# A recurrent attention kernel: the softmax weights of the first two units transposed by VectorE, dense rows laid out as 128 half rows

## The chip, the cores and the metric

The kernel runs on one core of a Trainium2 chip. The metric is the device time of one execution in microseconds, the median of several runs. A profile of one execution goes with it: TensorE is PE (its weight loads PEld), VectorE DVE, ScalarE ACT, GpSimd POOL, and SyncE SP, which issues most DMAs.

## The reference

Two layers of memory-augmented attention and two dense layers alternate, each behind a layernorm and with a residual, over 2048 rows of 512 (bf16):

```python
def _A_ref(x, mem0, Wq, Wk, Wv, Wo, seg_len):     # 32 heads of 128, 8 memory rows, segments of 32
    for s in range(n_seg):                         # 64 segments, one after the other
        h = jnp.concatenate([mem, xs], axis=1)     # 8 memory rows and 32 rows of the segment
        q, k, v = (jnp.einsum('btd,dhe->bhte', h, W) for W in (Wq, Wk, Wv))
        scores = jnp.einsum('bhqe,bhke->bhqk', q, k) * scale
        scores = jnp.where(mask[None, None], scores, -1000000000.0)
        p = _softmax(scores, axis=-1)
        o = jnp.einsum('bhqk,bhke->bhqe', p, v)
        o = jnp.einsum('bhte,hed->btd', o, Wo)
        mem = o[:, :M, :]                          # the next segment's memory
        outs.append(o[:, M:, :])
...
x = x + _A_ref(_layernorm(x), ...)
x = x + _B_ref(_layernorm(x), B_w1, B_w2)          # relu(x @ w1) @ w2, 512 to 1376 to 512
x = x + _A_ref(_layernorm(x), ...)
x = x + _B_ref(_layernorm(x), B_w1, B_w2)
```

The weights are the same in both passes. The memory ties each segment to the one before it.

## The kernel before, in words

The kernel walks in 66 steps. Step k works on segment k of the first attention layer and segment k - 2 of the second one at once (`DELTA` is 2), so that the 40 rows (8 of memory, 32 of the segment) of both stand side by side as 80 columns in `HT`. Steps 0, 1, 64 and 65 hold one layer only; 62 steps hold both.

In a step the 32 heads are cut into five units (`UNITS`): units 0 to 2 take eight heads each, units 3 and 4 four each. `queries_keys` forms q and k of four heads in 16 matmuls of 80 columns into a PSUM bank, and an eviction by ScalarE or VectorE brings them to SBUF as bf16. `scores` makes the 40 x 40 scores (matmuls of 40 columns in half the array's width), and then a chain runs: VectorE adds the mask (`block`, which also brings the scores out of PSUM), takes the maximum (`top`), subtracts it (`sub`), ScalarE applies the exponential, VectorE sums (`total`) and inverts (`recip`), and VectorE or GpSimd multiplies into the bf16 tile `P` (`mul`). PE transposes P against the identity (`turn`), and two masked evictions (`keep`, one for each half of the partitions, with the other half set to zero through `half`) write `PT`. `attend` multiplies PT with the values: those of the first layer in `V0`, of the second in `vw`. `project` sums all heads into one bank (`st`), and its eviction gives the next step's memory columns in `HT` and the rows `OX`.

`finish` takes the rows on. A DMA transpose on SP's queue turns OX into `y`; VectorE adds it to the residual `x` (`xg`), 64 rows of 512: 32 of each layer. `dense_layer` normalises them, turns them on PE (`turned`, four matmuls of 64 columns), runs w1 with the relu and w2. The totals give `Z`; its first 32 rows are normalised and turned for the second layer's HT two steps later, and kept as its residual (`carry`); its last 32 rows are the output (`narrow`, `store`). Row loads (`load_group`), late values of later groups (`prepare_late`, `late_values`) and copies of values into V0 (`place_values`) fill in between.

The order of all engines' instructions is worked out beforehand by a planner. `plan.op` names the engines an operation may run on, a cost for each, and what it reads and writes. PE's order is a list sorted by the numbers in `PLACE` (its phases: the first steps, the middle, the last ones); other operations get a due time from what follows them, shifted by `AHEAD`; and `Plan.order` gives each to the engine and place where it can start first. `PAIRED` names matmul groups that may run as two half-width halves, which saves a change of array width when their neighbours are half-width ones. Each engine's queue then runs in that order, and a late operation holds up all that stand behind it on its engine. In the change `PLACE`, `AHEAD`, `PAIRED` and `LOOK` have new values throughout, so nearly every instruction may change its place.

Of the kernel before, what the change touches and what calls it, by code (L numbers as in the profile page):

```python
# [8 lines left out]
BF = mybir.dt.bfloat16  # L9
# [21 lines left out]
LOOK = 0.0763052  # L31
PERIOD = 26.155362
PLACE = {
# [185 lines left out]


def t_dve(n, rate=1):
    return 0.07 + 1.042e-3 * n / rate


PART, MASKED = {ACT: 0.13, DVE: 0.10}, {ACT: 0.11, DVE: 0.065}
XBAR = 0.5, 0.2, 2.6


def t_pool(n):
    return 0.06 + 2.2e-3 * n  # L230

# [1144 lines left out]
```

## Time and profile before

| | before |
|---|---|
| median of 3 runs | 1590.69 us (1588.59 to 1592.59) |
| the profiled execution | span 1588.6 us, which is the fastest of the three runs |
| PE busy | 1569.5 us, 99% of the span |
| weight loads busy | 1411.1 us, 89% |
| DVE / ACT / POOL busy | 68% / 73% / 20% |
| granted TensorE clock | 0.998 of full |

An engine's busy time is the union of its instructions' spans. In a list of groups each line reads: source line, engine, operation, output <- input, shapes, count | busy us, mean ns of one | idle time just before, and what ended it. A matmul's shape carries the part of the array that it uses: 128*128 is the whole, 128*64 half its columns. In a timeline the first two columns are the start and the length of a merged group. In a table of stretches each engine has its busy us and its number of instructions, then come the granted clock, the DMA share and GB/s.

### The profile page before, as it was taken

Reading aid. Unit: us, or ns where it says so; the run is one execution under the profiler, and the core shown is the slowest. Engines: PE = TensorE matmul, PEld = TensorE weight load, DVE = VectorE, ACT = ScalarE, POOL = GpSimd, SP = SyncE. Lnnn points to the kernel's source line nnn. Section 1 sums busy time; section 2 is a strip of 40 time slices with the busy share of each in tenths; the row PEclk is TensorE's granted clock in tenths of the full one; section 3 lists DMA queues with packets and bytes.
Section 4 is the critical chain, followed back from the end, with each engine's and each line's share of the span. In section 5 each row is a group of like instructions: output and inputs, shape, how many; then the busy total and the mean of one; then the engine's idle time right before and its main releaser. Section 6 shows DMA issues by size and latency. Waiting matters only on the chain.

```text
span 1588.6 us, 100346 instructions
## 1 busy us (share of the span) xinstructions
PE 1569.5 (99%) x45458; PEld 1411.1 (89%) x45458; DVE 1082.3 (68%) x2957; ACT 1165.2 (73%) x3073; POOL 314.3 (20%) x667
## 2 busy tenths in 40 slices
PE   8999999999999999999999999999999999999998
PEld 5689999999999989999989999999998998898887
DVE  4566766766776776686676677677667667667665
ACT  4667777777777777777777777777777777777774
POOL 5112112212112212121121221211211121112110
PEclk9999999999999999999999999999999999999999
DMA  9711111111111111111111111111111111111100
GB/s 371 243 44 30 26 33 32 29 35 37 25 39 31 35 29 33 29 32 40 26 36 27 35 26 42 37 26 38 25 35 28 33 33 29 33 25 22 28 21 9
DMA packets 76540, 70.89 MB, mean 45 GB/s; under 512 B 50920, under 2 KB 62416, under 8 KB 76112
## 3 DMA queue, kind: packets, MB, share of 16 engines
q1 hardware_dynamic: 70096, 44.14, 13.1%
q0 software_dynamic: 4992, 19.40, 3.4%
q8 instruction: 356, 5.83, 1.6%
q10 hardware_dynamic: 1024, 0.93, 0.2%
q14 instruction: 72, 0.59, 0.1%
HBM read 31.53 MB, written 9.96 MB: 26 GB/s over the span
## 4 chain that ended last, share of the span: by engine, by line
PE 97%; DMA 1%; DVE 1%; POOL 1%; ACT 0%; issue 0%; DVEq 0%; POOLq 0%
PE work L726 40%; PE st L726 19%; PE fill L1048 16%; PE fill L726 8%; PE fill L821 5%; PE work L1217 5%; PE work L1133 4%; DMA xg<-in_A_x_dram 0%; DMA y<-OX 0%; DMA w_sb<-in_B_w_dram 0%; ACT HT L982 0%; POOL Wo_sb L537 0%; PE fill L711 0%; DVE ln L749 0%; POOL ln L736 0%
## 5 line engine op out<-in xcount | busy, mean ns | idle before, releaser
L726 PE MATMUL work<-HT,Wq_sb 128*128 128x80 bf16 (+2 forms) x10400 | 361.8, 201 | 3.1 <-ACT HT L982 3.1
L726 PE MATMUL work<-HT,Wk_sb 128*128 128x80 bf16 (+2 forms) x10416 | 362.7, 201 | 0.8 <-ACT HT L982 0.8
L726 PEld LDWEIGHTS <-Wq_sb 128*128 128x128 bf16 (+1 forms) x10400 | 330.9, 104 | 20.8 <-issue 6.0
L726 PE MATMUL st<-OT,Wo_sb 128*128 128x80 bf16 (+1 forms) x8448 | 345.5, 201 | 0.0
L726 PEld LDWEIGHTS <-Wk_sb 128*128 128x128 bf16 (+1 forms) x10416 | 327.1, 104 | 17.3 <-issue 2.0
L726 PEld LDWEIGHTS <-Wo_sb 128*128 128x128 bf16 x8448 | 315.7, 100 | 13.0 <-issue 12.7
L1048 PE MATMUL fill<-Wv_sb,HT 128*64 128x512 bf16 x2112 | 273.6, 381 | 1.1 <-DVE HT L984 1.0
L982 ACT CAST kT<-work 128x320 bf16<-128x320 f32 (+1 forms) x523 | 218.3, 418 | 68.6 <-PE work L726 31.1
L982 ACT CAST qT<-work 128x320 bf16<-128x320 f32 (+1 forms) x516 | 215.7, 418 | 67.5 <-PE work L726 47.2
L1198 ACT ACTIVATE PT<-work,half 128x160 bf16<-128x160 f32 (+1 forms) x515 | 231.3, 463 | 20.1 <-PE work L726 12.7
L982 ACT CAST OT<-work 128x320 bf16<-128x320 f32 (+1 forms) x461 | 186.2, 420 | 50.7 <-PE work L1217 50.6
L982 ACT CAST vw<-fill 128x512 bf16<-128x512 f32 x229 | 134.1, 586 | 113.3 <-PE fill L1048 109.8
L1144 DVE TENSOR_TENSOR es<-work,maskb 128x320 f32<-128x320 f32 (+2 forms) x330 | 136.2, 413 | 99.7 <-PE work L1133 93.2
L924 DVE TENSOR_TENSOR xg<-xg,y 64x512 f32<-64x512 f32 x65 | 44.2, 680 | 227.2 <-DMA y<-OX 226.6
L731 POOL TENSOR_SCALAR ln<-ln 32x1 f32<-32x1 f32 (+2 forms) x159 | 46.6, 293 | 566.7 <-DVE ln L752 561.0
L1155 ACT ACTIVATE es<-es 128x320 f32<-128x320 f32 (+2 forms) x330 | 136.1, 413 | 24.4 <-DVE es L1151 16.2
L1048 PEld LDWEIGHTS <-HT 128*64 128x64 bf16 x2112 | 98.9, 110 | 57.0 <-DVE HT L984 1.2
L1151 DVE TENSOR_TENSOR es<-es,mx 128x320 f32<-128x320 f32 (+2 forms) x330 | 136.3, 413 | 4.9
L1148 DVE TENSOR_REDUCE mx<-es 128x8 f32<-128x320 f32 (+2 forms) x330 | 133.9, 406 | 5.4
L1158 DVE TENSOR_REDUCE sm<-es 128x8 f32<-128x320 f32 (+2 forms) x330 | 133.4, 404 | 5.1 <-ACT es L1155 2.2
L1175 DVE TENSOR_TENSOR P<-es,sm 128x320 bf16<-128x320 f32 (+1 forms) x269 | 126.9, 472 | 3.3
L1133 PEld LDWEIGHTS <-qT 128*40 128x40 bf16 x4096 | 93.3, 97 | 35.6 <-ACT qT L982 13.6
(96 smaller groups left out, 2164.8 us busy)
## 6 DMA issues: line engine op xcount, KB each, us to landing
V<-vw SPq DMA_DIRECT2D x248, 48.0 KB
V<-vh SPq DMA_DIRECT2D x120, 64.0 KB
Wq_sb<-in_A_Wq_dram POOLq DMA_DIRECT2D x2, 2048.0 KB, 23.2
Wk_sb<-in_A_Wk_dram POOLq DMA_DIRECT2D x2, 2048.0 KB, 28.6
Wo_sb<-in_A_Wo_dram POOLq DMA_DIRECT2D x2, 2048.0 KB, 39.4
vh<-vg SPq DMA_DIRECT2D x32, 128.0 KB
xb<-in_A_x_dram SPq DMA_DIRECT2D x16, 128.0 KB
Wv_sb<-in_A_Wv_dram POOLq DMA_DIRECT2D x1, 2048.0 KB, 13.2
```

The costliest lines, as they stand in the source:

```text
L726: nc.tensor.matmul(out_[u:v, :], lhsT=lhsT[:, u:v], rhs=rhs, start=start, stop=stop, tile_position=(0, u), **more)
L821: nc.tensor.matmul(yp[64 * u:64 * u + 64, 0:256], lhsT=hT[:, fc, :], rhs=w2_sb[:, fc, 256 * u:256 * u + 256], start=(fc == 0), stop=(fc == ...
L982: nc.scalar.copy(out=out_, in_=in_)
L1048: nc.tensor.matmul(vp[64 * b:64 * b + 64, :], lhsT=cols(c4), rhs=Wv_sb[:, c4, n * 512:(n + 1) * 512], start=(c4 == 0), stop=(c4 == NC4 - 1 ...
L1133: nc.tensor.matmul(v[64 * g2:64 * g2 + L, a, i, b, :], lhsT=qT[:, hi, a * L:(a + 1) * L], rhs=kT[:, hi, a * L:(a + 1) * L], start=True, st ...
L1144: nc.vector.tensor_tensor(out=flat(es[:, A]), in0=flat(sp[:, A]), op=ALU.add, in1=maskb[:, a_lo:a_hi, :].unsqueeze(2).to_broadcast([128, n ...
L1148: nc.vector.tensor_reduce(out=mx[:, As], in_=es3(), axis=AX.X, op=ALU.max)
L1151: nc.vector.tensor_tensor(out=es3(), in0=es3(), op=ALU.subtract, in1=mx[:, As].unsqueeze(2).to_broadcast([128, ns * na, L]))
L1155: nc.scalar.activation(out=es[:, A], in_=es[:, A], func=ACTF.Exp, scale=SCALE)
L1158: nc.vector.tensor_reduce(out=sm[:, As], in_=es3(), axis=AX.X, op=ALU.add)
L1175: (nc.gpsimd if eng == POOL else nc.vector).tensor_tensor(out=o, in0=flat(es[:, A]), op=ALU.mult, in1=sm[:, As].rearrange("p (a s) -> p a ...
L1198: nc.scalar.activation(out=o, in_=i, func=ACTF.Copy, scale=half[:, b:b + 1])
```

## The change

- Units 0 and 1 (`BLOCKED`) are no longer transposed by PE. Their scores are stored so that the two heads of a pair alternate element by element; two bf16 make one 32-bit word. VectorE's `transpose` then turns blocks of 32 x 32 words from P into the unit's `es` buffer, and narrow copies (`stay`: 64 partitions; `shift`: two copies of 32 partitions that change their quarter) by ScalarE or GpSimd put the pieces into PT, whose other half stays zero from the start. The mask add reads the scores of a pair alternately; `mul` is two instructions; `attend` reads PT with a step of two elements.
- Units 2 to 4 keep the old way, into tiles named `PM`.
- The residual rows, y, Z and the dense rows are 128 half rows of 256 columns where they were 64 (or 32) rows of 512. The layernorm exchanges the two halves' statistics by two small copies (`swap`); the turns are two matmuls each; the copies `widen` and `carry` become two each, the totals one, the store two DMAs; the DMA transpose of OX has half the size.
- The row load of a group waits until the turn of OX has been issued (`("out", ...)`).
- `y`, `ob` and `xe` now lie in the free halves of `xg`, `none` and `mb0` in P tiles; `es` has three buffers instead of two; the mask has one copy for each pair.
- Two of the planner's POOL costs, and its tables, have new values.

```diff
-LOOK = 0.0763052
+LOOK = 0.1074729
...
+BLOCKED = (0, 1)
...
+def t_moved(eng, n):
+    return 0.205 + 0.86e-3 * n if eng == ACT else 0.20 + 1.08e-3 * n
...
-    PL = 256 + LK[1]
-    Pt = [sb(f"P{p}", [128, 2 * PL]) for p in range(4)]
+    PL = [256 + (2 if p in BLOCKED else 1) * LK[1] for p in range(4)]
+    Pt = [sb(f"P{p}", [128, 2 * PL[p]]) for p in range(4)]
...
+    spare = [t[:, 256:512].bitcast(BF) for t in xg]
+    p_y, p_ob, p_xe = Pool([spare[0][:, 0:256]]), Pool([spare[0][:, 256:512]]), Pool([spare[1]], True)
...
-    p_es = ring("es", 2, [128, 8 * L], F32)
-    p_PT = ring("PT", 3, [128, 2, 4, 2, L])
+    p_es = ring("es", 3, [128, 8 * L], F32)
+    p_PT, p_PM = ring("PT", len(BLOCKED), [128, 4, 2, 128]), ring("PM", 2, [128, 2, 4, 2, L])
...
-            plan.op(POOL, 0.80, power, r=["half"], w=[ln])
+            plan.op(POOL, 0.95, power, r=["half"], w=[ln])
...
+    def layernorm_halves(x, keys, quick=False):
+        ln, xn = p_ln.buf(), p_xr.buf()
+        R = slice(0, 128)
+        def stats():
+            nc.vector.bn_stats(out=ln[:, 0:6], in_=x[:, :])
+        def swap(eng):
+            for u in range(2):
+                copy_on(eng, ln[64 * u:64 * u + 64, 8:14], ln[64 - 64 * u:128 - 64 * u, 0:6])
+        def aggr():
+            nc.vector.bn_aggr(out=ln[:, 6:8], in_=ln[:, :].rearrange("p (s f) -> p s f", s=2)[:, :, 0:6])
+        def norm():
+            nc.vector.tensor_scalar(out=xn[:, 0:256], in0=x[:, :], scalar1=ln[:, 6:7], scalar2=ln[:, 7:8],
+                                    op0=ALU.subtract, op1=ALU.mult)
+        plan.op(DVE, t_dve(256), stats, r=keys, w=[ln])
+        plan.op((ACT, DVE), (0.2, 0.2), swap, w=[ln])
+        plan.op(DVE, 0.11, aggr, w=[ln])
+        rstd(ln, R, quick)
+        plan.op(DVE, 0.26, norm, r=[ln, *keys], w=[xn])
+        return xn
...
+    def turned(xn, n, columns, copies, blocks=NC4):
...
+            for c4 in range(blocks):
+                across(cols, tp[:, c4 * wide:(c4 + 1) * wide], xn[:, c4 * 128:(c4 + 1) * 128], columns)
...
-        xnT, xn = p_xm.buf(), layernorm(x, keys, slice(0, n), last)
-        turned(xn, n, ident[:, 0:n], [(NC4 * n, lambda: xnT[:, :, :], same, [], [xnT])])
+        xnT, xn = p_xm.buf(), layernorm_halves(x, keys, last)
+        turned(xn, n, ident[:, :], [(NC4 * n, lambda: xnT[:, :, :], same, [], [xnT])], 2)
...
-        plan.op(SP, 0.78, load, r=[("taken", 4 * g - 4)], w=[xb], lag=2.45)
+        plan.op(SP, 0.78, load, r=[("taken", 4 * g - 4), ("out", 4 * g - 4)], w=[xb], lag=2.45)
...
-            plan.op(SP, XBAR[0] + XBAR[1] * NC4, turn, r=["ox"], w=[y], lag=XBAR[2])
-        plan.op(DVE, t_dve(512), add, r=[y], w=keys)
+            plan.op(SP, XBAR[0] + XBAR[1] * 2, turn, r=["ox"], w=[y, ("out", k), *([("xv", 1), ("xv", 3)] if k == 0 else [])],
+                    lag=XBAR[2])
+        plan.op(DVE, t_dve(256), add, r=[y], w=keys)
...
+    def moved(eng, out_, in_):
+        if eng == ACT:
+            nc.scalar.copy(out=out_, in_=in_)
+        else:
+            nc.gpsimd.tensor_copy(out=out_, in_=in_)
 
...
-                            nc.tensor.matmul(v[64 * g2:64 * g2 + L, a, i, b, :], lhsT=qT[:, hi, a * L:(a + 1) * L],
+                for i in range(nx):
+                    for s in range(2):
+                        for t in range(2):
+                            g, b = (s, t) if blocked else (t, s)
+                            (qT, kT), hi = (qk[b], 2 * i + g) if nx == 2 else (qk[0], 2 * b + g)
+                            nc.tensor.matmul(v[64 * t:64 * t + L, a, i, s, :], lhsT=qT[:, hi, a * L:(a + 1) * L],
...
         def block():
-            nc.vector.tensor_tensor(out=flat(es[:, A]), in0=flat(sp[:, A]), op=ALU.add,
-                                    in1=maskb[:, a_lo:a_hi, :].unsqueeze(2).to_broadcast([128, na, ns, L]))
+            if blocked:
+                nc.vector.tensor_tensor(out=es[:, A].rearrange("p (j k s) -> p j k s", k=L, s=2), op=ALU.add,
+                                        in0=sp[:, A].rearrange("p (j s k) -> p j k s", k=L, s=2),
+                                        in1=maskb[:, mine, :].unsqueeze(3).to_broadcast([128, nj, L, 2]))
+            else:
+                o, i = (t[:, A].rearrange("p (j s k) -> p j s k", s=2, k=L) for t in (es, sp))
+                nc.vector.tensor_tensor(out=o, in0=i, op=ALU.add,
+                                        in1=maskb[:, mine, :].unsqueeze(2).to_broadcast([128, nj, 2, L]))
 
...
+        pieces = [(a, a + 1) for a in range(a_lo, a_hi)] if nx == 2 else [(a_lo, a_hi)]
+        def mul():
+            for a0, a1 in pieces:
+                o = P[:, :].rearrange("p (a c) -> p a c", a=2)[:, a0:a1, 128 * xs[0]:128 * (xs[-1] + 1)]
+                o = (o[:, 0, :] if nx == 2 else o).rearrange("p x (k g) -> p x k g" if nx == 1 else "p (x k g) -> p x k g", k=64, g=2)
+                j = slice((a0 - a_lo) * nx, (a1 - a_lo) * nx)
+                nc.vector.tensor_tensor(out=o[:, :, 0:L, :], in0=e_spread()[:, j, :, :], op=ALU.mult,
+                                        in1=by_head(sm)[:, j, :].unsqueeze(2).to_broadcast([128, nx * (a1 - a0), L, 2]))
+        plan.op(DVE, len(pieces) * (0.04 + t_dve(n / len(pieces))), mul, r=[es, sm], w=where)
         PT = p_PT.buf()
-        plan.op(PE, nx * na * 0.0358, turn, r=[*[("P", p, b, x) for b in range(2) for x in xs], "ident"], w=[tp, PT],
-                tile=EITHER, count=nx * na)
+        def turn():
+            nc.vector.transpose(out=es[:, 0:64 * nj].rearrange("p (j k) -> p j k", k=64),
+                                in_=P[:, 0:512].bitcast(F32).rearrange("p (j k) -> p j k", k=64)[:, mine, :])
+        def turned_pairs():
+            return es[:, 0:64 * nj].rearrange("p (j k) -> p j k", k=64), PT[:, 0:nj, :, :].bitcast(F32)
+        plan.op(DVE, 0.09 + 1.06e-3 * 64 * nj, turn, r=[*where, "PT0"], w=[es, PT])
         for b in range(2):
...
+            def stay(eng, b=b):
+                i, o = turned_pairs()
+                R = slice(64 * b, 64 * b + 64)
+                moved(eng, o[R, :, b, 0:L], i[R, :, 0:L])
+            def shift(eng, b=b):
+                i, o = turned_pairs()
+                for c, w in ((0, L - 32), (1, 32)):
+                    R, T = slice(64 * b + 32 * c, 64 * b + 32 * c + 32), slice(64 * b + 32 - 32 * c, 64 * b + 64 - 32 * c)
+                    moved(eng, o[R, :, b, 32 - 32 * c:32 - 32 * c + w], i[T, :, 32 * c:32 * c + w])
+            plan.op((ACT, POOL), (t_moved(ACT, L * nj), t_moved(POOL, L * nj) + 0.07), stay, r=[es, PT], w=[(PT, b)])
+            plan.op((ACT, POOL), tuple(t_moved(e, (L - 32) * nj) + t_moved(e, 32 * nj) for e in (ACT, POOL)), shift,
+                    r=[es, PT], w=[(PT, b)])
...
+        def spread(a, i, g):
+            if p in BLOCKED:
+                return PT[:, (a - a_lo) * nx + i, :, :].rearrange("p b (q g) -> p b q g", g=2)[:, :, 0:L, g]
+            return PT[:, a, 2 * i + g, :, :]
 
...
-                                             rhs=PT[:, a, 2 * i + h2, :, :], start=True, stop=True, tile_position=(0, u))
+                                             rhs=spread(a, i, h2), start=True, stop=True, tile_position=(0, u))
```

More of the change, by code (lines that the diff above doesn't have):

```diff
@@ L692, in prepare, with zero_last @@
         plan.op(DVE, 0.12, keep, r=[tp], w=["mem0T"])
+        def zero_last():
+            nc.vector.memset(Pt[2][:], 0.0)
+        plan.op(DVE, 0.30, zero_last, w=[mb0, *[("P", 2, b, x) for b in range(2) for x in range(2)]])
         plan.op(DVE, 0.12, place, r=["mem0T"], w=[("HTm", 0)])
@@ L902, in finish @@
         last = k == nsteps - 1
[L903 removed]
+        x, keys = x_of[k % 2], [("x", k % 2, a) for a in range(2)]
         if 0 in act:
@@ L937, in total @@
         def total(to):
-            for u in range(2):
-                cs = slice(256 * u, 256 * u + 256)
-                nc.vector.tensor_tensor(out=to[RB, cs], in0=x[RB, cs], in1=yp[64 * u:64 * u + 64, 0:256], op=ALU.add)
+            nc.vector.tensor_tensor(out=to[:, :], in0=x[:, :], in1=yp[:, 0:256], op=ALU.add)
         def total_x():
@@ L1193, in scores @@
-        for b in range(2):
-            def keep(eng, b=b):
-                o = PT[:, a_lo:a_hi, 0:2 * nx, b, :]
-                i = tp[:, A].rearrange("p (a g q) -> p a g q", g=2 * nx, q=L)
-                if eng == ACT:
-                    nc.scalar.activation(out=o, in_=i, func=ACTF.Copy, scale=half[:, b:b + 1])
-                else:
-                    nc.vector.tensor_scalar_mul(out=o, in0=i, scalar1=half[:, b:b + 1])
-            copy_op(n, keep, r=[tp, PT, "half"], w=[(PT, b)], more=MASKED)
+        where = [("P", p, b, x) for b in range(2) for x in xs]
```

269 lines of the change are left out of this document (146 added, 123 removed), and 231 rows, old and new, of tables (PAIRED, PLACE).

## The prediction

> **What bounds the kernel now.** The page comes first: parts 1 and 4, then the stretches, then one step in order of time.
>
> ```profile
> span 1588.6 us, 100346 instructions
> PE 1569.5 (99%) x45458; PEld 1411.1 (89%) x45458; DVE 1082.3 (68%) x2957; ACT 1165.2 (73%) x3073; POOL 314.3 (20%) x667
> PE 97%; DMA 1%; DVE 1%; POOL 1%; ACT 0%; issue 0%; DVEq 0%; POOLq 0%
> ```
> ```profile
> 0.00:24.00 24.00, 17.68 (x140) 10.04 (x142) 9.79 (x32) 8.37 (x15) 14.36 (x33) 0.86 0.94 354
> 400.00:600.00 200.00, 200.00 (x5888) 182.97 (x5883) 140.51 (x378) 151.76 (x400) 38.56 (x83) 1.00 0.15 31
> ...
> 800.00:1000.00 200.00, 200.00 (x5897) 183.01 (x5894) 142.27 (x383) 152.06 (x401) 41.11 (x87) 1.00 0.15 32
> ...
> 1560.00:1589.00 29.00, 24.13 (x724) 20.83 (x723) 14.80 (x52) 12.96 (x44) 1.32 (x3) 1.00 0.05 10
> ```
>
> PE carries 97% of the chain that ends last, and in the steady stretches it is busy for all 200 us of 200, at full granted clock. A busy PE is not proof of a full one, since matmuls overlap; the starts in the next fence are. Column 1 is the start, and the next group's start minus this one's, over the count, is what one matmul costs.
>
> ```profile
> 788.04 0.26 PE L726 MATMUL fill<-ident,xr 128*128 128x32 bf16 x4
> 788.15 0.73 PE L726 MATMUL st<-OT,Wo_sb 128*128 128x80 bf16 x16
> ...
> 792.61 1.31 PE L726 MATMUL work<-HT,Wk_sb 128*128 128x80 bf16 x32
> 793.86 0.37 PE L1133 MATMUL work<-kT,qT 128*40 128x40 bf16 x16
> ```
> ```profile
> 801.07 0.28 PE L726 MATMUL fill<-ident,xr 128*128 128x64 bf16 x4
> 801.19 0.74 PE L726 MATMUL work<-HT,Wq_sb 128*128 128x80 bf16 x16
> 801.76 0.45 PE L726 MATMUL work<-ident,P 128*128 128x80 bf16 x8
> 802.08 1.09 PE L726 MATMUL fill<-xnM,w_sb 128*128 128x64 bf16 x32
> 803.01 0.74 PE L726 MATMUL work<-HT,Wk_sb 128*128 128x80 bf16 x16
> ...
> 805.99 0.31 PE L726 MATMUL work<-ident,P 128*64 128x80 bf16 x8
> 806.13 0.21 PE L1217 MATMUL work<-PT,V 128*64 128x80 bf16 x2
> ```
>
> So: 80 columns cost 0.57/16 = 35.6 ns, 64 columns (w1) 0.93/32 = 29.1, a turn of P 0.32/8 = 40, a turn of 64 columns 0.12/4 = 30, of 32 columns 0.11/4 = 27.5. In half width (128*64) eight turns of P take 0.14, 17.5 each, 35 the pair: the same. The 32 matmuls before the scores take 1.25 where 32 x 35.6 is 1.14: a change of width costs about 0.10. No group waits. Work taken from PE is therefore time saved, as long as nothing else comes late.
>
> **The change on PE.** Counts are from the order of the two built programs.
>
> ```profile
> L726 PE MATMUL work<-ident,P 128*128 128x80 bf16 x756 | 59.3, 202 | 0.2 <-DVE P L1175 0.2
> L726 PE MATMUL work<-ident,P 128*64 128x80 bf16 x536 | 22.0, 201 | 0.4 <-DVE OT L984 0.4
> ```
>
> - Turns of P: 756 whole and 268 pairs become 256 whole and 256 pairs. 500 whole at 35.6 to 40 and 12 pairs at 35 give -18.2 to -20.4 us. I take -19.3, the middle, since the 40 holds the entry into the group.
> - Turns of the second layernorm's rows: 256 of 32 columns become 128 of 64: 128 x 30 - 256 x 27.5 = -3.2.
> - Turns of the dense rows: 264 of 64 columns (7.9 us) become 132 of 128. A column costs (35.6 - 29.1)/16 = 0.41, so one is 29.1 + 64 x 0.41 = 55 ns, 7.3 us: -0.6.
> - The re-planned order puts 680 more w1 matmuls into half-width pairs. At 80 columns pair and whole are equal, so the low end is 0; at most a pair of 64 columns costs what one of 80 does, +6.5 ns: 0 to +4.4. I take +1.
> - Changes of width: 299 become 293, -0.6. The other counts on PE stay (attend 2048 halves and 1024 wholes before, 2056 and 1020 after).
>
> Together -22.7, with ends -18 and -25. The last step's dense part is bare. There the add and the statistics of 512 columns (0.68 us each in the rows below) become 256 columns, near the 0.40 of a 256-column total, and the two totals become one; the exchange of statistics adds two small operations: -0.8.
>
> **The change beside PE.**
>
> ```profile
> L1200 DVE TENSOR_SCALAR PT<-work,half 128x320 bf16<-128x320 f32 x121 | 65.9, 545 | 0.3
> L940 DVE TENSOR_TENSOR vx<-xg,fill 64x256 f32<-64x256 f32 x128 | 51.6, 403 | 3.1 <-PE fill L821 1.8 <-PE work L1217 0.3
> L749 DVE BATCH_NORM_STATS2 ln<-xg 64x6 f32<-64x512 f32 x66 | 44.7, 678 | 0.5
> L924 DVE TENSOR_TENSOR xg<-xg,y 64x512 f32<-64x512 f32 x65 | 44.2, 680 | 227.2 <-DMA y<-OX 226.6
> L1144 DVE TENSOR_TENSOR es<-work,maskb 128x320 f32<-128x320 f32 x186 | 90.8, 488 | 67.4 <-PE work L1133 67.2
> L1144 DVE TENSOR_TENSOR es<-work,maskb 128x160 f32<-128x160 f32 x136 | 43.7, 321 | 27.6 <-PE work L1133 21.3
> L1175 DVE TENSOR_TENSOR P<-es,sm 128x160 bf16<-128x160 f32 x75 | 34.2, 455 | 0.2
> L984 DVE CAST OT<-work 128x320 bf16<-128x320 f32 x59 | 29.0, 491 | 34.8 <-PE work L1217 34.8
> L1161 DVE RECIPROCAL sm<-sm 128x4 f32<-128x4 f32 x136 | 21.8, 161 | 0.2
> ```
> ```profile
> L1198 ACT ACTIVATE PT<-work,half 128x320 bf16<-128x320 f32 x251 | 133.1, 533 | 0.0
> L1198 ACT ACTIVATE PT<-work,half 128x160 bf16<-128x160 f32 x263 | 97.8, 396 | 19.7 <-PE work L726 12.3
> ```
> ```profile
> L1175 POOL TENSOR_TENSOR P<-es,sm 128x160 bf16<-128x160 f32 x61 | 27.7, 454 | 150.2 <-DVE sm L1161 150.2
> L998 POOL COPY HT<-xnA 128x128 bf16<-128x128 bf16 x63 | 18.4, 292 | 477.2 <-PE work L726 453.4 <-PE fill L1048 23.7
> ```
>
> DVE pays (488 - 321)/160 = 1.04 ns a column here. It gains 132 transposes (256 columns, between the rows of 160 and 320, so about 0.42: +55), 136 exchanges (like the 161 ns reciprocal: +22) and 160 evictions of q, k and OT that ACT had (0.49: +78). It loses 121 turn evictions of 320 columns for some 65 of 160 (0.545 and about 0.38: -41), 62 relus of 256 and 29 evictions of vw of 512 columns (0.42 and 0.69 by the column: -46), and in each step 0.26 for the add and for either statistics and 0.39 for the totals (1.17 x 64 = -75); half norms and fewer whole products I leave at nothing. It ends no busier than 68%. ACT loses some 128 + 80 masked evictions (-100) and those 160, and gains 247 narrow copies at 0.2 to 0.4 and 62 relus: no busier than 73%. POOL gains 497 narrow copies (0.2 to 0.35, +130), 61 products of 320 columns and halves of row copies: about 500 us, 32%. SP has one more store a step, ahead of the V loads:
>
> ```profile
> SPq L1068 <- PE work L1217: 139.8, 62, 8.4
> ```
>
> SP waits 2.3 us a step there, and a second store of under 1 us hides in it; uncovered it would delay the turn of OX, and so the dense rows. The tiles that now share memory (y, ob and xe in the free halves of xg) add no order in the steady steps: each stays a single buffer with the users it had. A row load queued behind that turn is used some two steps later, so its wait costs nothing.
>
> One cost is not hidden: what comes late next. Rows of one unit's softmax:
>
> ```profile
> 800.18 0.38 PE L1133 MATMUL work<-kT,qT 128*40 128x40 bf16 x16
> 800.60 0.49 DVE L1144 TENSOR_TENSOR es<-work,maskb 128x320 f32<-128x320 f32 x1
> 801.01 0.48 DVE L1175 TENSOR_TENSOR P<-es,sm 128x320 bf16<-128x320 f32 x1
> 801.41 0.48 DVE L1148 TENSOR_REDUCE mx<-es 128x8 f32<-128x320 f32 x1
> 801.92 0.49 DVE L1151 TENSOR_TENSOR es<-es,mx 128x320 f32<-128x320 f32 x1
> ...
> 804.30 0.49 DVE L1175 TENSOR_TENSOR P<-es,sm 128x320 bf16<-128x320 f32 x1
> ```
>
> DVE starts an independent operation of 320 columns every 0.41 us, a dependent one after 0.51. Now the third unit's P is ready at 804.79, and PE turns it at 805.99: 1.2 us to spare. After, the first two units' scores stand together, about 12 us into the step, and 17 DVE operations precede the third unit's first: 10 of 320 columns or near (4.1), four half products (1.2), two reciprocals (0.4), a transpose (0.4), about 0.3 of waiting for the exponential: 6.4 us from 12.3, so 18.7, where now it is 17.7. The second transpose falls inside the unit's chain (+0.4), and its product goes to POOL: 320 columns by the 454 ns row some 0.8 us against 0.49. 1.2 - 1.0 - 0.4 - 0.3 is about -0.5; evictions and relus that DVE does now between 801 and 804 and then mostly not give back about 0.4. I take 0.12 us late, in 62 full steps: +7.5, with ends 0 and 0.5 x 62 = 31.
>
> Sum: 1588.6 - 22.7 - 0.8 + 7.5 = 1572.6 for the profiled execution. That is 2.1 below the 1590.7 median of the three runs, so the forecast is 1575; its own range 1563 to 1585.
>
> **The rivals.** First, the lateness eats the gain. It does when P of the third unit, or a narrow copy, comes 0.38 us late per step (23.5/62). For it: the thin sum above, and DVE and POOL disturb each other: the product of 160 columns takes DVE 455 ns, where the mask add of that size takes 321 and POOL's own product beside it 454. The Trainium skill ("GPSIMD Engine Reference", Key points) says that GpSimd shares its SBUF interfaces with VectorE; that row agrees. Against: much of the new POOL work meets reductions and PSUM evictions. 0.3 to 0.5 late: 1585 to 1598.
>
> Second, slower: the first two units' mask add now reads its scores from PSUM with a step of 40 elements. Nothing in the trace reads so. At 1.04 ns a column, if each is fetched twice, an add is 0.33 longer, the two 0.67, ahead of the third unit on the same queue. All of it on PE is 62 x 0.67 = 41 us, 1616; half is 1596; it decides from the same 0.38. The Trainium skill ("Advanced Engine Details and Errata", Memory Cachelines) speaks for it: PSUM has 8-byte lines, and every two consecutive elements should be contiguous. It says so of matmuls, and no run here shows it; without this rule I would halve its chance.
>
> Third, slower: attend streams the transposed pairs with every second element, 1024 whole matmuls' worth for the two units. At half speed that is 1024 x 35.6 = +36 us, 1611. The nearest rows stream contiguous columns at full rate. The skill's same section wants two hits on a 16-byte SBUF line, and a step of two elements has four; by it this costs nothing.
>
> **How the numbers follow.** A measurement of this kernel can tell about 0.3%, 4.8 us: faster is below 1586, slower above 1595.5. Forecast 0.64; gain eaten 0.15 (0.04 faster, 0.06 same, 0.05 slower); PSUM step 0.13; streaming 0.08. Faster 0.68, same 0.06, slower 0.26. The range runs from 1562 (no lateness, the turns of P at their dear end) to 1604, which takes in the eaten gain and the PSUM step at half its price and leaves out about 0.17.
>
> **What would show it.** Right: ident,P falls to 256 whole and 512 halves, PE is still busy 200 of 200, the step 0.3 us shorter, attend at 36 ns. Wrong: an idle before ident,P of the third unit ended by POOL; mask adds of the first two units near 0.8 us; attend of these units at 70 ns; or an idle before attend ended by a narrow copy.

## The result, and the profile after

| | before | after |
|---|---|---|
| median, side by side on one chip | 1589.72 us (18 runs) | 1592.22 us (18 runs) |
| ratio | | 1.0016 (95% interval 1.0009 to 1.0023) |
| profiled execution, span | 1588.6 us | 1590.6 us |
| DVE / ACT / POOL busy | 68% / 73% / 20% | 64% / 74% / 32% |

The change made no difference that counts: 0.16%, and if anything slower. The forecast was 1575 us, so 17 us that were expected did not come. (In every other run here the span is 1.7 to 1.9 us shorter than the measured time of the same execution. So the span of 1588.6 us of before most likely belongs to an execution near its median, not to the fastest of its three runs, and the two spans in the table can be compared.) The first lines of the page of the changed kernel, and from its part 4 the engines' shares of the chain:

```profile
span 1590.6 us, 101922 instructions
PE 1566.3 (98%) x45454; PEld 1403.1 (88%) x45454; DVE 1024.2 (64%) x3237; ACT 1177.5 (74%) x3189; POOL 516.1 (32%) x1384
PE 90%; ACT 3%; DVE 2%; issue 1%; POOL 1%; DMA 1%; SPq 0%; POOLq 0%; DVEq 0%; ACTq 0%
```

One of the stretches that were shown of before (start and end, length, then PE's busy us):

```profile
400.00:600.00 200.00, 199.49 (x5892) 180.78 (x5887) 132.64 (x417) 153.89 (x416) 66.75 (x180) 1.00 0.14 29
```

PE's share of the chain fell from 97% to 90%: ScalarE, VectorE and GpSimd now stand in it for 6%. The busy columns hide that. A matmul is drawn about 200 ns long and one starts every 36, so PE looks busy through any wait shorter than some 160 ns; in 200 us, which are 8.5 steps with 0.57 us of waits each, only 0.5 us of them shows. The Trainium skill ("Perfetto Trace Analysis", Identifying the Most-Contended Engine) says that matmul busy time is no good measure of how close a kernel is to its limit, because matmuls are pipelined; this trace agrees (199.5 of 200 us busy, in a kernel that lost its gain to waits).

The waits become visible from the starts. For every run of equal matmuls in PE's order I took the distance to the start of the next run and subtracted the count times the usual cost of that kind (35.8 ns for 80 columns, half of that in half width, 0.10 us for a change of width). What is left, summed between 100 and 1500 us (59 steps), is called "waits" below:

| kernel | mean step | PE's work in 59 steps | waits in 59 steps |
|---|---|---|---|
| before | 23.491 us | 1374.6 us | 11.4 us |
| after | 23.512 us | 1353.8 us | 33.4 us |

(The mean step is the distance between the starts of the output projections of steps 3 and 62, over 59; the work is the steps less the waits.) PE's work fell by 20.8 us, near the forecast, and the waits rose by 22.0. (With the usual costs taken a little otherwise either figure moves by 1 to 1.5 us; their difference is fixed by the steps.) The gain was made, and given back in many pieces, most of them of 30 to 330 ns. The largest are ahead of the attend of units 0 and 1 (1.0 us before, 4.4 after), inside that attend (3.7), and ahead of the fourth unit's output projection (5.4); they make about 12.5 of the 22 us, and the rest lies in smaller pieces.

One step of the changed kernel: PE's queue, then ScalarE's and GpSimd's just before it:

```profile
782.73 0.27 PE L1190 MATMUL work<-kT,qT 128*40 128x40 bf16 x8
782.85 0.55 PE L742 MATMUL fill<-xnM,w_sb 128*64 128x64 bf16 x24
783.23 0.27 PE L1190 MATMUL work<-kT,qT 128*40 128x40 bf16 x8
783.41 0.23 PE L1332 MATMUL work<-PT,V 128*64 128x80 bf16 x2
```
```profile
782.00 0.32 ACT L1035 COPY PT<-es 64x160 f32<-64x160 f32 x1
782.34 0.47 ACT L1226 ACTIVATE es<-es 128x320 f32<-128x320 f32 x1
782.72 0.41 ACT L1029 CAST kT<-work 128x320 bf16<-128x320 f32 x1
```
```profile
782.38 0.54 POOL L1037 COPY PT<-es 32x32 f32<-32x32 f32 x2 [0.41 <-PE work L742]
```

The same eight score matmuls take 0.12 us at 782.73 and 0.18 at 783.23. So PE waits some 60 to 80 ns. The narrow copies were done by 782.92 (the last are GpSimd's two). The step's last key eviction was not: it stands on ScalarE behind a narrow copy and the exponential, ends at 783.13, and frees the bank that the attend writes. (That it is this one is shown below, where it is moved.)

In 11 of the 59 steps a longer wait, of some 0.32 us, comes inside the attend, and the chain of waits names it (start, length, what):

```profile
828.97 0.47 ACT es L1226
...
829.47 0.33 ACT PT L1035
...
829.92 0.21 POOL PT L1037
...
830.17 0.30 POOL PT L1037
...
830.51 0.48 PE work L1332 x16
```

Here a straight narrow copy stands behind the exponential on ScalarE, GpSimd's shift of the same piece must follow it, and half of the attend waits for that.

The third place: VectorE and GpSimd ahead of the projection of the fourth unit, and PE.

```profile
765.04 0.57 DVE L796 TENSOR_SCALAR xr<-vx,ln 128x256 bf16<-128x256 f32 x1 [0.85 <-POOL ln L752]
765.53 0.48 DVE L1031 CAST OT<-work 128x320 bf16<-128x320 f32 x1
```
```profile
763.15 0.89 POOL L1002 COPY xg<-vx 32x256 f32<-32x256 f32 x2
764.13 0.22 POOL L747 TENSOR_SCALAR ln<-ln 128x1 f32<-128x1 f32 x1
764.44 0.57 POOL L752 TENSOR_TENSOR ln<-ln,mhalf 128x1 f32<-128x1 f32 x1
```
```profile
765.88 0.20 PE L1332 MATMUL work<-PM,vw 128*128 128x80 bf16 x1
766.06 0.73 PE L742 MATMUL st<-OT,Wo_sb 128*128 128x80 bf16 x16
```

VectorE's queue holds the normalisation of the second layernorm ahead of the eviction of the fourth unit's attend (in the order of before it is the other way round). The normalisation waits 0.85 us for GpSimd, which is behind its own copies; the eviction ends at 766.01, and PE starts the projection at 766.06 where 765.91 was due.

### The profile page after: what moved, and what is told of

Read it like the earlier page. It is cut to its first block, busy times and chain, and to the rows that moved or that the text cites. A ratio compares the mean times of both kernels' runs of the same rounds, so it can differ in the third digit from the quotient of the medians.

```text
span 1590.6 us, 101922 instructions
## 1 busy us (share of the span) xinstructions
PE 1566.3 (98%) x45454; PEld 1403.1 (88%) x45454; DVE 1024.2 (64%) x3237; ACT 1177.5 (74%) x3189; POOL 516.1 (32%) x1384
## 4 chain that ended last, share of the span: by engine, by line
PE 90%; ACT 3%; DVE 2%; issue 1%; POOL 1%; DMA 1%; SPq 0%; POOLq 0%; DVEq 0%; ACTq 0%
PE work L742 36%; PE st L742 19%; PE fill L1101 16%; PE fill L742 7%; PE work L1332 5%; PE fill L864 5%; PE work L1190 3%; ACT PT L1035 1%; ACT es L1226 1%; DMA V<-vw 1%; ACT kT L1029 0%; DMA xb<-in_A_x_dram 0%; DVE es L1223 0%; ACT hT L852 0%; DVE mx L1213 0%
## 5 line engine op out<-in xcount | busy, mean ns | idle before, releaser
L1037 POOL COPY PT<-es 32x32 f32<-32x32 f32 (+4 forms) x521 | 156.1, 300 | 350.7 <-PE work L1190 164.3
L1029 ACT CAST qT<-work 128x320 bf16<-128x320 f32 (+1 forms) x452 | 188.8, 418 | 82.4 <-PE work L742 50.0
L1029 ACT CAST kT<-work 128x320 bf16<-128x320 f32 (+1 forms) x479 | 199.1, 416 | 42.9 <-PE work L742 4.5
L1029 ACT CAST vw<-fill 128x512 bf16<-128x512 f32 x258 | 151.2, 586 | 90.6 <-PE fill L1101 88.1
L747 POOL TENSOR_SCALAR ln<-ln 128x1 f32<-128x1 f32 x159 | 35.4, 223 | 524.2 <-DVE ln L793 408.5
L1029 ACT CAST OT<-work 128x320 bf16<-128x320 f32 (+1 forms) x399 | 152.6, 418 | 40.4 <-PE work L1332 39.3
L1270 ACT ACTIVATE PM<-work,half 128x160 bf16<-128x160 f32 (+2 forms) x317 | 133.8, 442 | 34.1 <-PE work L742 32.2
L1223 DVE TENSOR_TENSOR es<-es,mx 128x320 f32<-128x320 f32 (+2 forms) x330 | 150.8, 469 | 1.8
L742 PE MATMUL fill<-xnM,w_sb 128*128 128x64 bf16 (+1 forms) x3668 | 119.3, 194 | 0.7 <-ACT xnM L1029 0.5
L1204 DVE TENSOR_TENSOR es<-work,maskb 128x320 f32<-128x320 f32 (+1 forms) x132 | 59.0, 476 | 94.2 <-PE work L1190 91.4
```

Source lines behind the costliest of these rows:

```text
L742: nc.tensor.matmul(out_[u:v, :], lhsT=lhsT[:, u:v], rhs=rhs, start=start, stop=stop, tile_position=(0, u), **more)
L1029: nc.scalar.copy(out=out_, in_=in_)
L1037: nc.gpsimd.tensor_copy(out=out_, in_=in_)
L1223: nc.vector.tensor_tensor(out=e_spread(), in0=e_spread(), op=ALU.subtract, in1=i1)
L1270: nc.scalar.activation(out=o, in_=i, func=ACTF.Copy, scale=half[:, b:b + 1])
```

## The experiments

Theory A: the gain went into waits for the narrow copies. Theory B: it went into the queues of VectorE, ScalarE and GpSimd in general. Theory C: a fixed cost at the new attend. Ratios are to the kernel before, measured on the same chip. A difference to the changed kernel is one of medians from two chips, on which the kernel before differed by less than 1 us where its time is on record. "Waits" is the sum defined above.

### Is work taken from PE time saved?

The kernel before, with three of the four turns of P of units 0 and 1 left out (the quarter-turns run):

```diff
             for a in range(a_lo, a_hi):
                 for i, x in enumerate(xs):
+                    if p < 2 and z_last != nx * a + i:
+                        continue
```

> The kernel before, with three of the four TensorE turns of P of each of the first two units left out (some 372 matmuls; the order, the evictions and every other operation stay; the attend of these units reads old columns of the bank). If work taken from TensorE is time saved, as the prediction had it, the time falls by 372 x 35.6 to 40 ns = 13 to 15 us. If the order of before is so tight that whatever is taken from TensorE comes back as waits for the other engines, it falls by less than half of that, under 7 us.

Measured: 1589.62 us, ratio 1.0000 (0.9990 to 1.0009). Nothing, with 385 matmuls fewer. The waits rose from 11.4 to 24.0 us, and the whole rise is at one place, ahead of w1: 14.3 us, 0.246 in each step, where it was 31 ns a step before. The chain of waits of this run:

```profile
776.98 0.52 PE work L726 x14
...
777.57 0.43 ACT kT L982
778.00 0.28 ACT xnM L982
...
778.32 0.69 PE fill L726 x18
```

w1 waits for the eviction of xnM, which stands on ScalarE behind a key eviction. The turn of the dense rows starts at 777.31 in this run and w1 at 778.32: 1.01 us. In the rows of before it is 801.07 to 802.08: also 1.01. So this handover (turn on PE, eviction on ScalarE, w1 on PE) had no more work laid over it than it needs, and whatever is taken out of that work comes back as a wait.

Next, the same kernel with one more projection between that turn and w1:

```diff
+        i, j = key_at(q, "dense_layer.mm.da.0", k), key_at(q, "queries_keys.mmu4.1", k + 1)
+        ...
+            q.insert(i, q.pop(j))
```

> As the quarter-turns run (the kernel before with three of four TensorE turns of P of the first two units left out), and on TensorE the last key projection of the step goes ahead of the first two w1 groups, so that 16 more matmuls (0.57 us) stand between the turn of the dense rows and w1. In the quarter-turns run w1 waited 0.246 us in each of 59 steps, which is what the turns had cost. If the saving was lost only to that handover (turn of the dense rows, eviction, w1: 1.01 us from start to start in both runs), the wait goes and the time falls by 12 to 15 us below before. If the next handover takes its place, it falls by less than half of that.

Measured: 1594.22 us, 1.0035 (1.0022 to 1.0048), slower. The wait ahead of w1 is gone and another of 0.283 us in each step has come: my exchange put three w1 groups next to each other, and the third waits for VectorE's relu (0.44 us at 759.51 in that chain) of an earlier one. It says that handovers stand close together, not that PE's time is worth nothing.

Then, with PE's order left as it was, two neighbours exchanged on ScalarE:

```diff
+        if q[j].key == "turned.keep.da.0" and q[j - 1].key == "queries_keys.evu3.1":
+            q[j - 1], q[j] = q[j], q[j - 1]
```

> As the quarter-turns run (before, with three of four TensorE turns of P of the first two units left out), and on ScalarE the eviction of xnM goes ahead of the key eviction of the fourth unit, which it stood behind: in that run w1 waited 0.246 us a step for it. If TensorE's saving is lost only to that place in the queue, the time falls by 12 to 15 us below before. If VectorE and ScalarE bound the step as closely as TensorE does, most of the wait turns up at another place: less than 7 us.

Measured: 1575.00 us, ratio 0.9909 (0.9894 to 0.9924): 14.6 us less than before, for 385 matmuls. ScalarE's queue of this run and PE's:

```profile
769.25 0.37 ACT L982 CAST xnM<-fill 128x256 bf16<-128x256 f32 x1 [0.40 <-PE fill L726]
769.52 0.43 ACT L982 CAST kT<-work 128x320 bf16<-128x320 f32 x1
```
```profile
768.93 0.28 PE L726 MATMUL fill<-ident,xr 128*128 128x64 bf16 x4
769.05 0.74 PE L726 MATMUL work<-HT,Wq_sb 128*128 128x80 bf16 x16
769.62 0.24 PE L726 MATMUL work<-ident,P 128*128 128x80 bf16 x2
769.69 0.69 PE L726 MATMUL fill<-xnM,w_sb 128*128 128x64 bf16 x18
```

From turn to w1 it is now 0.76 us, and the waits are 11.1. Work taken from PE is worth its full price here, and one place in another engine's queue was enough to take all of it away. The complete kernel before with that exchange alone:

> The kernel before, complete, with the eviction of xnM ahead of the key eviction of the fourth unit on ScalarE. The wait ahead of w1 was 31 ns in 59 steps there: 0 to 2 us faster. More than 4 us would mean that the kernel before had waits that the matmul starts don't show.

Measured: 1589.31 us, 0.9993 (0.9984 to 1.0002): no difference beyond what can be told. The 31 ns ahead of w1 are gone in its trace, where the same eight turns of P take 0.28 us instead of 0.32:

```profile
801.71 0.45 PE L726 MATMUL work<-ident,P 128*128 128x80 bf16 x8
801.99 1.10 PE L726 MATMUL fill<-xnM,w_sb 128*128 128x64 bf16 x32
```

So the order of before was cut to fit its own work: a wait of 31 ns there, and no slack. The mean step is 23.479 us here and 23.265 with the quarter turns and the same exchange: 0.214 us for six turns, 35.7 ns each, which is the usual cost of 80 columns.

### The narrow copies or the queues?

The changed kernel, with the attend of units 0 and 1 reading a constant:

```diff
-                return PT[:, (a - a_lo) * nx + i, :, :].rearrange("p b (q g) -> p b q g", g=2)[:, :, 0:L, g]
+                return Wo_sb[:, 0, 0:256].rearrange("p (b q g) -> p b q g", b=2, g=2)[:, :, 0:L, g]
```

> The changed kernel, where the attend matmuls of the first two units read a constant stretch of the output weights with the same step of two elements, and not the turned pairs; transposes and narrow copies still run. Left out: the true values of these two units, and with them TensorE's wait for the narrow copies. Theory A (the gain went into waits for the narrow copies): the waits ahead of and inside this attend, some 8 of the 22 us that the changed kernel waits more, go, and the time falls by 6 to 9 us. Theory B (the waits come from the crowded queues of VectorE, ScalarE and GpSimd in general): only the rare long waits inside the group go, 2 to 4 us. Theory C (a fixed cost on TensorE at this place, whatever is waited for): less than 2 us.

and with the narrow copies left out as well (`moved` returns at once):

> As the run with the constant attend, and the narrow copies themselves are left out too, so GpSimd loses some 3.4 us a step and ScalarE some 1.2 us; VectorE's transposes stay. Theory A: no more than 2 us below the constant attend. Theory B: the queues are the cause, so 5 us or more below it, near the 21 us of TensorE work that the change took away (1570 to 1578 us). Theory C: the same as the constant attend within 2 us, and both near the changed kernel.

Measured: 1598.11 us (1.0051, 1.0036 to 1.0066) and 1586.15 us (0.9976, 0.9967 to 0.9986). Neither total can be read as it stands: the constant lay in the output weights, which land late, and the first 100 us held 1598 and 1615 matmuls where the changed kernel has 1811 (step 3 starts its projections at 133.0 and 131.5 us instead of 126.3). The steps can be read. With the constant a step takes 23.495 us instead of 23.512 (1.0 us in 59 steps, as theory C had it and less than theories A and B), and the wait ahead of the attend stays, so that wait is not for the narrow copies; only the one inside the attend goes, and waits behind it grow, the one ahead of the fourth unit's projection from 5.4 to about 6.5 us. Without the copies a step takes 23.323 and both waits at the attend are gone. The last run was repeated with a constant from the key weights, and there step 3 starts at 126.4:

> The no-narrow run again (no narrow copies, constant attend of the first two units), with the constant taken from the key weights, which arrive earlier than the output weights: in the two runs before, the first 100 us had some 200 fewer matmuls, since the first steps waited for that constant. Theory B: 1576 to 1581 us, 11 to 16 below the changed kernel. If the slow start had another cause, 1585 again.

Measured: 1581.37 us, 0.9951 (0.9936 to 0.9966), 10.9 us below the changed kernel, at the edge of what theory B had; waits 22.5. Theory A falls as it was put: of the 22 us, PE's own wait for the copies is the 3.7 inside the attend. Theory C falls too, since the wait ahead of the attend goes with the copies. Nor do the copies cost by slowing VectorE: its subtraction of 160 columns takes 463 ns in the mean in this run and 465 in the changed kernel. What is left is the time that the copies take in the queues, ahead of evictions that PE needs.

Is VectorE's queue the bound, which is full from about the 13th microsecond of a step on? The row maximum of all units left out, in either kernel:

```diff
         def top():
+            if 4 <= k < 62:
+                return
```

> The changed kernel, with the row maximum of all five units left out from the fifth step on (the subtraction takes an old maximum): VectorE loses 1.7 us a step in the stretch where its queue is full, TensorE, ScalarE and GpSimd keep their work. If VectorE's queue is what holds TensorE up, the waits go: 1570 to 1580 us. If the waits come from ScalarE's queue or from the narrow copies alone, at most 5 us: 1587 to 1592.

> The kernel before with the same row maximum left out. TensorE has no room there, so 1587 to 1591 us, no change, if TensorE alone bounds it. If VectorE is a bound of its own in before, more than 5 us.

Measured: 1589.50 us (1.0001, 0.9992 to 1.0010) and 1589.24 us (0.9998, 0.9988 to 1.0007). Of the changed kernel's page:

```profile
PE 1563.5 (98%) x45454; PEld 1401.9 (88%) x45454; DVE 947.5 (60%) x2947; ACT 1174.6 (74%) x3189; POOL 512.5 (32%) x1384
```

VectorE lost 77 us of busy time, and the kernel 2.7 us; the wait ahead of the attend is still 79 ns. VectorE's load is not what holds PE up. For VectorE theory B can be right only in a narrower form: not how much its queue holds, but in which order. Whether order is enough on the other engines too is what the next runs ask.

### Order alone

Each of these runs is the complete changed kernel with neighbours exchanged or moved in the queues beside PE. First the normalisation and the eviction behind it:

```diff
+        for j, o in enumerate(order):
+            if o.key == "layernorm_halves.norm.db.0":
+                i = next(i for i in range(j + 1, len(order)) if order[i].eng == DVE)
+                if order[i].key == "attend.evu3.0":
+                    order[j:i + 1] = order[j + 1:i + 1] + [o]
```

> The changed kernel with one pair of VectorE's queue exchanged in 56 steps: the first attend eviction of the fourth unit goes ahead of the normalisation of the second layernorm, which waits 0.85 us for GpSimd, as in the order of before. The trace of the changed kernel has a wait ahead of the projection of the fourth unit, 5.4 us in all. If the eviction behind that normalisation causes it, the time falls by 4 to 5.5 us; if the projection waits for something else, or the turn of the normalised rows is then late, by less than 1.5 us.

Measured: 1588.70 us, 0.9991 (0.9982 to 1.0000), 3.5 below the changed kernel, a little less than expected. The wait ahead of the fourth unit's projection is gone; one of 48 ns ahead of the fifth's has come (2.8 us). It fits that the turn of the normalised rows between the two projections is now two matmuls (0.06 us) instead of four (0.11), but no run tests it.

The last key eviction to VectorE:

```diff
+        if None not in (j, t) and d[t - 1].start < a[j].start < d[t].start:
+            d.insert(t, a.pop(j))
```

(`a` is ScalarE's queue, `d` VectorE's, and `t` the place of the third unit's sum.)

> The changed kernel, where in 50 steps the last key eviction of a step goes from ScalarE, where it stands behind the second narrow copy and the exponential, to VectorE, which is idle for 0.55 us there. Theory B (crowded queues): the attend of the first two units waits some 83 ns for the bank that this eviction frees, and the scores of the fifth unit 30 ns for the keys; both go, 5 to 7 us. Theory A (the narrow copies themselves): no change, within 1.5 us. A third outcome: VectorE gives the 0.4 us back as a later third unit, 0 to 5 us slower.

Measured: 1591.80 us, 1.0018 (1.0008 to 1.0027): nothing, the total that theory A had. But the trace shows that the wait moved: the one ahead of the attend of units 0 and 1 fell from 4.4 to 0.6 us, as theory B had it, and the one ahead of the third unit's attend rose from 1.9 to 5.2.

Both of these exchanges, and in 10 steps the straight narrow copy to GpSimd:

```diff
+        if None not in (j, x, s) and j > x:
+            p.insert(s + 1, a.pop(j))
```

(`j > x`: the copy stands behind the exponential; `p` is GpSimd's queue, `s` the place of the first unit's first shift.)

> The changed kernel with three changes of the queues beside TensorE: the attend eviction ahead of the normalisation (the run before gave 3.5 us), the last key eviction on VectorE (5 to 7 us by theory B), and in the 10 steps in which the first unit's last straight narrow copy stands behind the exponential on ScalarE that copy on GpSimd, behind the first unit's shift (0.33 us each, 3 us). By theory B the sum is 9 to 13 us: 1579 to 1583 us, faster than both kernels. By theory A the last two bring less than 4 us together: 1585 to 1589.

Measured: 1588.52 us, 0.9993 (0.9984 to 1.0002), what the first exchange had given alone; theory B as it was put had 1579 to 1583. PE and ScalarE in this run:

```profile
786.52 0.25 PE L742 MATMUL work<-ident,P 128*128 128x80 bf16 x2
786.70 0.20 PE L1332 MATMUL work<-PM,V 128*128 128x80 bf16 x1
```
```profile
785.36 0.53 ACT L1270 ACTIVATE PM<-work,half 128x320 bf16<-128x320 f32 x1
785.90 0.34 ACT L1226 ACTIVATE es<-es 128x160 f32<-128x160 f32 x1
786.14 0.51 ACT L1270 ACTIVATE PM<-work,half 128x320 bf16<-128x320 f32 x1
```

Two turns take 0.18 us where 0.07 is usual: the third unit's attend waits for the second eviction of its P, which stands behind an exponential that waits for VectorE. So two more: that eviction ahead of that exponential, and the last shift on GpSimd ahead of a copy of rows.

```diff
+        if q[j].key == "scores.keepu2.1" and q[j - 1].key == "scores.expu4.0":
+            q[j - 1], q[j] = q[j], q[j - 1]
...
+            p.insert(s + 2, p.pop(key_at(p, "scores.shiftu0.1", k)))
```

> The run with three changes of queues, and two more: on ScalarE the second eviction of the third unit's turned P goes ahead of the exponential of the fifth unit (the attend of the third unit waited 0.105 us a step for it), and in the 10 steps in which the last narrow copy stood behind a copy of rows on GpSimd it goes ahead of it (0.3 us). If order alone takes the waits away: 1579 to 1584 us, faster than both kernels. If the queues are simply full there, the wait moves on: 1586 to 1589, as with three.

Measured: 1582.61 us, 0.9955 (0.9939 to 0.9972): 9.6 us below the changed kernel and 7.0 below the one before, faster than both. A step takes 23.345 us, the waits are 24.1, and the chain is PE's again:

```profile
PE 95%; DVE 1%; POOL 1%; issue 1%; ACT 1%; DMA 0%; SPq 0%; POOLq 0%; DVEq 0%; ACTq 0%
```
```profile
783.11 0.24 PE L742 MATMUL work<-ident,P 128*128 128x80 bf16 x2
783.21 0.20 PE L1332 MATMUL work<-PM,V 128*128 128x80 bf16 x1
```

The two turns take 0.10 us. Is it that last exchange alone?

> The changed kernel with one exchange alone: on ScalarE the second eviction of the third unit's turned P ahead of the exponential of the fifth unit. If the waits stand in a row (taking one away lets the next grow) and this one is the later of two, it brings little by itself, since the wait ahead of this attend is only 31 ns there, a bare handover: within 1.5 us of the changed kernel. If the waits are independent, it brings what it brought beside the others, 3 to 6 us.

Measured: 1592.55 us, 1.0014 (1.0004 to 1.0023): nothing. And with the key eviction on VectorE, but the normalisation where the change put it?

> The changed kernel with two exchanges: the last key eviction on VectorE (alone: nothing) and that eviction of P ahead of the exponential. If the two waits are one chain, both together bring what the first wait was, 4 to 6 us below the changed kernel: 1586 to 1588. If not, nothing again: 1590 to 1592.

Measured: 1593.61 us, 1.0018 (1.0008 to 1.0028): nothing, against what I expected. Both waits are down to 0.6 and 1.4 us there, and the one ahead of the fourth unit's projection has grown from 5.4 through 7.0 (the last exchange alone) to 9.3. So three waits stand in a row, and the last of them, behind the normalisation that waits for GpSimd, takes up what PE wins ahead of it. Of the three exchanges run alone, the one at the normalisation is the only one that brought something; the six microseconds more of the five came when the eviction of P and the last shift were added to three. Which of the five are needed is not shown: no run leaves out one of them.

## Why the prediction was wrong, point by point

- **The step that failed is the term for lateness.** "I take 0.12 us late, in 62 full steps: +7.5", with 31 as the far end: 22.0 us more waits were measured in 59 steps, 0.37 us a step. The term came from one chain, the third unit's P behind GpSimd's product, and there no such wait came, but for one step. The waits came at other places: the attend of units 0 and 1, for a key eviction that stands on ScalarE behind a narrow copy and the exponential; inside that attend, for narrow copies (the sign "ended by a narrow copy" that the prediction had named); the third unit's attend, for an eviction of P behind an exponential (1.9 us, and 5.2 once the first of these waits was gone); and the fourth unit's projection, for VectorE's eviction behind the second layernorm's normalisation. Of the last one the prediction left the half norms "at nothing" and looked at no neighbour in the queue. Of the 18.0 us between the 1572.6 forecast for the profiled execution and its 1590.6, this term is 14.5.
- **"No group waits" was false too.** The fence that carried it held the contrary: eight turns of P took 0.32 us, 40 ns each, where half-width pairs came to 35, and the prediction called the rest "the entry into the group". It was a wait of 31 ns in every step for the eviction of xnM, gone where that eviction goes first. It said that this handover had no slack left; the quarter-turns run lost its whole saving to it. In the changed kernel this handover is not among the places that wait; it shows on the kernel before what happens elsewhere in the changed one. What followed, "work taken from PE is time saved, as long as nothing else comes late", holds only with its second half: 14.6 us with one exchange of two evictions, nothing without it.
- **The saving on PE was right.** 256 whole turns and 512 halves are left, as counted:

```profile
L742 PE MATMUL work<-ident,P 128*128 128x80 bf16 x256 | 30.9, 202 | 1.0 <-DVE P L1248 1.0
L742 PE MATMUL work<-ident,P 128*64 128x80 bf16 x512 | 22.4, 201 | 0.1
```

  20.8 us in 59 steps, 21.9 in 62, against -22.7 forecast; a turn left out is worth 35.7 ns, and 38.6 was taken. From step 62 to the end of PE's last matmul it is 1.1 us shorter (74.13 to 73.01), but what follows that matmul is 0.6 longer (3.53 to 4.09), so the end as a whole is 0.6 shorter, against -0.8. The start up to step 3 is 1.4 longer (124.91 to 126.32), for which the sum had no term; two of the runs with exchanged queues stand at 126.85 and 128.18 there, so this part varies by about as much.
- **The sums of busy time beside PE came out nearly (VectorE 64% where at most 68% was said, ScalarE 74% where at most 73%, GpSimd 32% as said), and decided nothing.** VectorE another 4 points emptier, without the row maximum, brought 2.7 us.
- **First rival, the lateness eats the gain:** it is what happened, near its threshold: 0.38 us a step was named, 0.37 came (22.0/59). It had 0.15. It should have had more: the re-planned order touched nearly every instruction, and the prediction checked one chain.
- **Second rival, PSUM read with a step of 40 elements:** false.

```profile
L1204 DVE TENSOR_TENSOR es<-work,maskb 128x320 f32<-128x320 f32 x124 | 56.5, 486 | 85.5 <-PE work L1190 82.7 <-ACT vw L1029 2.7
```

  486 ns, where the plain add of before took 488. The Trainium skill's rule on PSUM lines ("Advanced Engine Details and Errata", Memory Cachelines) speaks of matmuls; carried over to this read of VectorE's it did not hold.
- **Third rival, attend at half speed:** false. The 32 half-width attend matmuls of a step take from 783.41 to 784.00, 18.4 ns each, where half of 35.6 is 17.8. The same section of the Trainium skill, on SBUF lines, had it so.
- **VectorE and GpSimd disturb each other:** right, and larger than taken. In the changed kernel the subtraction of 160 columns takes 465 ns in the mean where it took 320:

```profile
L1223 DVE TENSOR_TENSOR es<-es,mx 128x160 f32<-128x160 f32 x136 | 63.1, 465 | 0.1
```
```profile
L1151 DVE TENSOR_TENSOR es<-es,mx 128x160 f32<-128x160 f32 x136 | 43.5, 320 | 2.3
```

  The Trainium skill ("GPSIMD Engine Reference", Key points) names the shared interfaces; these rows agree. The cost fell on the chain to the exponential of the fourth unit. The row that the prediction gave for it was read in part wrongly: none of VectorE's 75 products of 160 columns in the trace of before runs beside a product of GpSimd's. 62 run beside GpSimd's copy of rows (32x512) and take 484 ns in the mean; the 9 that run beside nothing take 320.

Still open: the last 7.6 us between 1582.6 and the forecast. Waits of 24.1 us remain in the best version against 11.4 before, among them the 48 ns a step ahead of the fifth unit's projection, which another order on PE might cover; that was not tried. Nor was the dense part of the change run without the transposes, so its own share is known only from the counts.

## What to carry to other kernels

- Before time taken from the busiest engine is counted as saved, look for the waits too short for the busy column: distances between starts, run by run, against the usual cost. A handover that takes exactly as long as the work laid over it shows as "no wait" and has no slack, and a saving inside that work is lost to it.
- Waits on an engine that works in order can stand in a row. Taking one away lengthened the next here, up to the last one of the row. Begin with that one, and judge such repairs together: two of the single ones and a pair brought nothing, and five together 9.6 us.
- How busy an engine is says little about whether it is late. Ask what stands directly ahead of each operation that the busiest engine waits for, above all one that itself waits.

## What the runs showed of the hardware that I had not expected

GpSimd's work slows VectorE by the kind of operation on either side. GpSimd's and VectorE's queues of the changed kernel:

```profile
783.82 0.72 POOL L1248 TENSOR_TENSOR P<-es,sm 128x320 bf16<-128x320 f32 x1 [0.55 <-ACT hT L852]
```
```profile
783.60 0.32 DVE L1213 TENSOR_REDUCE mx<-es 128x4 f32<-128x160 f32 x1
783.83 0.32 DVE L1209 TENSOR_TENSOR es<-work,maskb 128x160 f32<-128x160 f32 x1
784.07 0.66 DVE L1223 TENSOR_TENSOR es<-es,mx 128x160 f32<-128x160 f32 x1
```

The mask add, with one input in PSUM, takes its usual 0.32 us beside that product. The subtraction, with both inputs in SBUF, takes 0.66 instead of some 0.31. The whole trace says the same: 61 subtractions of 160 columns beside such a product take 654 ns in the mean and the 75 others 311, while 62 mask adds beside it take 316 and the 74 others 315. GpSimd's narrow copies do not slow VectorE so: the 62 subtractions of 320 columns that run beside one take 481 ns, those beside nothing 484. A product moved to GpSimd gives part of its time back on VectorE if an operation that it slows runs beside it.
